# The calls for the third batch's loads moved, in pairs, between the first output stores, and ACT's token-order copies on every second quarter of an output tile

## The chip, the cores and the metric

The kernel runs on one core of a Trainium2 chip. The metric is device time in microseconds (us), lower is better; faster or slower asks for 2%. Engines: PE is TensorE (PEld its weight loads), ACT is ScalarE, DVE is VectorE, POOL is GpSimd, SP is SyncE. "ACTq" and "SPq" are the instruction queues of ACT and SP where they issue DMAs. L304 means line 304 of the kernel.

## The reference

Sliding-window attention (window 32, 8 batches, 8 heads, 576 tokens, head size 64), then two matrix products with a leaky ReLU between:

```python
scores = scale * np.matmul(q, k.transpose(0, 1, 3, 2))      # (8, 8, 576, 576)
scores = np.where(np.abs(pos[:, None] - pos[None, :]) <= 32, scores, -1e9)
attn = softmax(scores)                                      # cut: written out in the reference
x = np.matmul(attn, v).transpose(0, 2, 1, 3).reshape(4608, 512)
h = x @ w_in                                                # (4608, 2048)
out = np.maximum(0.01 * h, h) @ w_out                       # (4608, 512) float32
```

## The kernel before

Attention goes in 64 steps (8 batches x 2 halves of the tokens x 4 pairs of heads), and the two products go on beside it: a hidden group of 16 tiles (`h_tile`, 288 tokens) and output tiles (`o_tile`, 128 tokens) follow each other on TensorE, and a plan says before which hidden tile or quarter of an output tile the next attention step is put. So TensorE is fed all the time, as long as no attention step has to wait.

Parts that matter, with cuts marked by `# ...`. The loads, one buffer for each pair of heads:

```python
    def load_qk(b, p, behind=None):
        for into, src, name in ((qf, q, "qf"), (kf, k, "kf")):
            t = fload.tile([96, 2, RUN * D], FP32, name=f"{name}{p}")
            # ...
            nc.sync.dma_start(out=t, in_=src[b, p:H:NPAIR].rearrange("a (p c) d -> p a (c d)", c=RUN))
            into[b, p] = t
    # load_v(b, p): two DMAs of 144 KB, likewise on nc.sync, into vf{p}
```

The token-order copies. From batch 5 on (`BY_DMA = 5`) a DMA transposes q and k, and ACT puts the result into token order; DVE then places the keys (`place_keys`, L226):

```python
                tok = tp.rearrange("p c i -> p i c")
                if which == "q":
                    nc.scalar.activation(out=qT[b][:, p].rearrange("p (i c) -> p i c", c=RUN), in_=tok, func=AF.Copy)   # L208
                else:
                    kT = kt.tile([128, S], BF16, name="kT")
                    # ...
                    nc.scalar.activation(out=kT_v, in_=tok, func=AF.Copy)                                               # L214
                    unplaced.append((b, p, kT))
```

An attention step. `score` for step i+2: PE writes `ps` (one PSUM buffer), ACT takes the exponential `e` (L247), POOL masks it. `join(i+1)` is two small DVE instructions (L262, L264). `weighted(i)`: PE sums into `s` (L273) and multiplies into `x` (L285), DVE takes the reciprocal `r` (L291) and multiplies into `xT` (L293), which the hidden group reads:

```python
        if JOINED - 1 <= i < NC - 1:
            join(i + 1)
        place_keys()
        # ... transposes for the next batch
            score(i + 2)
        weighted(i)
        place_keys()
```

An output tile, with a hook before each quarter; ACT copies the result out of PSUM and issues the store itself:

```python
            # ... o: a PSUM tile; lo, hi: its columns, all 512 but in the last tile
            for f in range(FFC):
                if hook and lo == 0 and f % 4 == 0:
                    hook()
                nc.tensor.matmul(o[:, lo:hi], gT[:, f, ds(128 * j % RING, 128)], w_out_bf[:, f, lo:hi], ...)
            o_sb = outp.tile([128, DMODEL], FP32, name="o_sb")
            nc.scalar.activation(out=o_sb[:, lo:hi], in_=o[:, lo:hi], func=AF.Copy)      # L326
            nc.scalar.dma_start(out=out[ts(j, 128), lo:hi], in_=o_sb[:, lo:hi])          # L327
```

The plan's loop, where the change is:

```python
    for p in range(NPAIR):
        load_qk(2, p)                    # ahead of the first output tile
    # ...
    cast_v(1, 0)
    load_v(2, 0)

    def spend(us):
        nonlocal clock
        while due and due[0] <= clock:
            due.pop(0)
            i = state["done"]
            if i < 11:
                cast_v(1, i - 7)
                load_v(2, i - 7)
            step()

        b, p = state["tp"] // 8, state["tp"] % 8 // 2
        if kind == "o" and b >= BY_DMA and (b, p, "k") in qkT and state["done"] > 8 * b - 12 + p + 2:
            step_transposes(state["tp"] + 1)      # one token-order copy
            place_keys()
        clock += us
```

The framework that the kernel is written in gives DMAs issued from SP and ACT eight completion semaphores in rotation. A DMA therefore carries a wait until the eighth DMA before it has landed, counted over both engines, in the order in which the framework's scheduler expects them to issue. That is read from the built program's waits, and it concerns the program, not the chip. Below, q0, k0, v0 and so on are the third batch's loads of head pair 0 (a v load is two DMAs), and "batch 5" counts from 0.

The softmax here doesn't subtract the row's maximum and nothing guards it: scores larger than these inputs give would overflow.

Of the kernel before, what the change touches and what calls it, by code (L numbers as in the profile page):

```python
# [16 lines left out]
def kernel(  # L17
# [20 lines left out]
    NPAIR = H // 2  # L38
# [25 lines left out]
# [5 lines that stand above are left out]
            if behind is not None:  # L69
                nc.sync.dma_start(out=t[0:1, 0, 0:1], in_=behind.bitcast(FP32))  # L70
                behind = None
            nc.sync.dma_start(  # L72
                out=t, in_=src[b, p:H:NPAIR].rearrange("a (p c) d -> p a (c d)", c=RUN),
            )
            into[b, p] = t

    def load_v(b, p, behind=None):

        t = fload.tile([128, NB, D], FP32, name=f"vf{p}")
        if behind is not None:  # L80
            nc.sync.dma_start(out=t[0:1, 0, 0:1], in_=behind.bitcast(FP32))
        for a in range(2):
            nc.sync.dma_start(  # L83
                out=t[64 * a:64 * a + 64],
                in_=v[b, NPAIR * a + p].rearrange("(c p) d -> p c d", p=64),
            )
        vf[b, p] = t
# [78 lines left out]
    def cast_qk(b, p, q_eng=None):  # L166
        for eng, src, dst in ((q_eng or nc.gpsimd, qf, qb), (nc.gpsimd, kf, kb)):
            eng.tensor_copy(  # L168
                out=dst[:, p], in_=src[b, p].rearrange("p a (c d) -> p c a d", d=D),
            )  # L170

    def cast_v(b, p, on_act=False):
        for a in range(2):
            r = slice(64 * a, 64 * a + 64)
            if on_act:
                nc.scalar.activation(out=vbd[b % 2][r, p, :, r], in_=vf[b, p][r], func=AF.Copy)
            else:
                nc.gpsimd.tensor_copy(out=vbd[b % 2][r, p, :, r], in_=vf[b, p][r])  # L178


    BY_DMA = 5
    qkT = {}

    def transpose_dma(b, p):
        for which, src in (("q", qb), ("k", kb)):
            t = tdma.tile([128, RUN, 96], BF16, name=f"{which}T{p}")
            nc.sync.dma_start_transpose(out=t, in_=src[:, p].rearrange("p c a d -> p (c a d)"))
            qkT[b, p, which] = t
# [31 lines left out]
    def place_keys():  # L220

        while unplaced:
            b, p, kT = unplaced.pop(0)
            for a in range(2):
                r = slice(64 * a, 64 * a + 64)
                nc.vector.tensor_copy(  # L226
                    out=kbd[b % 2][r, p, :, r],
                    in_=kT[r].rearrange("p (n j) -> p n j", j=64),
                )
# [3 lines left out]
    def where(i):  # L233
        return i // 8, (i // 4) % 2, i % 4

    def score(i):
        b, hf, p = where(i)
        ps = scps.tile([128, 1024], FP32, name="ps")
        c0 = 512 - HALF
        for blk, q0, n in WIN[hf]:  # L240
            nc.tensor.matmul(  # L241
                ps[:, c0:c0 + n], kbd[b % 2][:, p, blk],
                qT[b][:, p, q0:q0 + n], start=True, stop=True,
            )
            c0 += n
        e = attn.tile([128, NCOL], BF16, name="e")
        nc.scalar.activation(  # L247
            out=e, in_=ps[:, 512 - HALF:512 - HALF + NCOL], func=AF.Exp, scale=scale,
        )
        pr = prob.tile([128, NCOL], BF16, name="pr")  # L250
        nc.gpsimd.tensor_mul(pr, e, mask[hf])  # L251
        probs[i] = pr, None

    def join(i):


        hf = where(i)[1]
        pr = probs[i][0]
        both = prob.tile([128, HALF], BF16, name="both")
        o0 = ODD[hf]  # L260
        o1 = o0 + NCOL - HALF
        nc.vector.tensor_add(both[:, o0:o1], pr[:, o0:o1], pr[:, HALF:NCOL])  # L262
        rest = slice(0, o0) if o0 else slice(o1, HALF)
        nc.vector.tensor_copy(out=both[:, rest], in_=pr[:, rest])  # L264
        probs[i] = pr, both

    def weighted(i):
        b, hf, p = where(i)
        pr, both = probs.pop(i)
        x = xps.tile([128, HALF], FP32, name="x")  # L270
        s = xps.tile([128, HALF], FP32, name="s")
        if both is not None:
            nc.tensor.matmul(s, ones_bd, both, start=True, stop=True)  # L273
        else:
            nc.tensor.matmul(
                s, ones_bd, pr[:, 0:HALF], start=True, stop=False, skip_group_check=True,
            )
            nc.tensor.matmul(
                s[:, ODD[hf]:ODD[hf] + NCOL - HALF], ones_bd, pr[:, HALF:NCOL],
                start=False, stop=True, skip_group_check=True,  # L280
            )
        c0 = 0
        for n_, (blk, q0, n) in enumerate(WIN[hf]):
            a = q0 - HALF * hf
            nc.tensor.matmul(  # L285
                x[:, a:a + n], vbd[b % 2][:, p, blk, :], pr[:, c0:c0 + n],
                start=(n_ == 0), stop=(n_ == len(WIN[hf]) - 1), skip_group_check=True,
            )
            c0 += n
        r = attn.tile([128, HALF], FP32, name="r")  # L290
        nc.vector.reciprocal(r, s)  # L291
        t0 = (b * S + hf * HALF) % RING
        nc.vector.tensor_mul(xT[:, p, t0:t0 + HALF], x, r)  # L293
# [45 lines left out]
    state = {"tp": 8, "done": 0}  # L339
# [12 lines left out]
    def step_transposes(upto):  # L352
        while state["tp"] < min(upto, 8 * B):
            b = state["tp"] // 8
            if b not in t_parts:
                t_parts[b] = transposes(b)
            next(t_parts[b])
            state["tp"] += 1

    def step():  # L360


        i = state["done"]
        b, r = i // 8, i % 8
# [3 lines that stand above are left out]
        if b > 0:  # L368
            upto = 8 * (b + 1) + (PLAN[b > 1][0][r] if b + 1 < BY_DMA else 0)
            step_transposes(max(upto - 1, 8 * (b + 1)))  # L370
        if i < 7:
            score(i + 1)
        elif 8 <= i < NC - 2:
            nb, _, np_ = where(i + 2)
            if nb >= BY_DMA:
                step_transposes(8 * nb + 2 * np_ + 2)
# [4 lines that stand above are left out]
        if b > 0:  # L381
            step_transposes(upto)
        if 0 < b < B - 1:
            for p in PLAN[b > 1][1][r] if b + 1 < BY_DMA else ():
                cast_qk(b + 1, p)
                if b + 2 < B:
                    load_qk(b + 2, p)

            n, p = (b + 1, 3) if r == 0 else (b + 2, r - 4)
            if p in range(4 if r == 0 else 3) and BY_DMA <= n < B:  # L390
                step_transposes(8 * (n - 1) + 2 * p + 2)
                place_keys()
                cast_qk(n, p)
                transpose_dma(n, p)
                if n + 1 < B:
                    load_qk(n + 1, p)
            for p in PLAN[b > 1][2][r]:
                cast_v(b + 1, p)
                if b + 2 < B:
                    load_v(b + 2, p)  # L400
        state["done"] += 1
# [70 lines left out]
    for f in range(FFC):  # L472
        h_tile(1, f)
        if f % 4 == 3:
            p = f // 4
# [7 lines left out]
            score(8)  # L483
    state["tp"] = 16
    score(9)
    for p in range(NPAIR):
        load_qk(2, p)



# [18 lines left out]
        due.append(prev + (at[i // 4] - LEAD + (1.2 if i < 12 else 0) - prev) * (i % 4 + 1) / 4)  # L509
    clock = 0.0  # L510
    cast_v(1, 0)
    load_v(2, 0)

    def spend(us):
        nonlocal clock
        while due and due[0] <= clock:
            due.pop(0)
            i = state["done"]
            if i < 11:
                cast_v(1, i - 7)  # L520
                load_v(2, i - 7)
            step()

        b, p = state["tp"] // 8, state["tp"] % 8 // 2
        if kind == "o" and b >= BY_DMA and (b, p, "k") in qkT and state["done"] > 8 * b - 12 + p + 2:
            step_transposes(state["tp"] + 1)
            place_keys()
        clock += us

    for us, kind, g, f in plan:  # L530
        if kind == "h":
            spend(us)
            h_tile(g, f)
        elif f == 0:
            o_tile(g, lambda: spend(O_US))
# [28 lines left out]
```

## Time and profile before

| | before |
|---|---|
| time, median of 3 runs | 336.55 us (336.29 to 337.34) |
| span of the profiled run | 336.1 us (it took 337.79 us, mean granted clock 0.990) |
| PE busy | 314.5 us (94%) |
| DVE, ACT, POOL busy | 228.3, 213.9, 180.5 us |
| PE idle between 40 and 315 us | 5.5 us in three gaps |

No engine but PE is near its limit as an average, and yet PE's few gaps are made by others. The way to read this profile is to find the gaps of PE and ask at each which instruction it waited for, and what that one stood behind. The prediction below shows those lines and how they are read.

### The profile page before, as it was taken

The page shows a single profiled execution, that of the slowest core. Times are in us where ns is not written, and L with a number is a line of the kernel's source. Part 1 is how long each engine was busy: PE and PEld are TensorE (multiplying, and loading weights), DVE is VectorE, ACT ScalarE, POOL GpSimd, SP SyncE. Part 2 cuts the span into 40 slices and gives each one's busy share as a digit, 9 for nine tenths or more (in the row PEclk, how much of TensorE's full clock was granted, in tenths as well). Part 3 has the DMA queues.
Part 4 walks back from the last instruction along what each step waited for, and adds up shares of the span by engine and source line. Part 5 has one row for each costly group of instructions (what it writes and reads, how often), then busy time and mean ns, then how long its engine had stood idle before and what let it go on. Part 6 is the DMA issues. An engine that isn't in the chain of part 4 may idle for free.

```text
span 336.1 us, 6770 instructions
## 1 busy us (share of the span) xinstructions
PE 314.5 (94%) x2581; PEld 210.8 (63%) x2581; DVE 228.3 (68%) x310; ACT 213.9 (64%) x432; POOL 180.5 (54%) x213
## 2 busy tenths in 40 slices
PE   2588999699999999999999799999999999999996
PEld 1346775376675767667675475748585666666653
DVE  5489654598777978888676867777786767666200
ACT  5775792266674756667489587878787555555441
POOL 6797767549764646659541666529741454221000
PEclk9999999799999999999999899999999999999999
DMA  8999978997695433568993289914840101010102
GB/s 187 219 196 225 269 179 187 258 196 200 186 191 169 124 71 115 150 196 154 221 184 103 82 158 226 211 50 113 145 117 34 62 2 62 2 63 3 62 2 93
DMA packets 75445, 45.93 MB, mean 137 GB/s; under 512 B 54292, under 2 KB 70932, under 8 KB 75412
## 3 DMA queue, kind: packets, MB, share of 16 engines
q1 hardware_dynamic: 65796, 31.86, 46.3%
q10 hardware_dynamic: 5328, 9.44, 8.1%
q0 software_dynamic: 4288, 4.20, 7.6%
q8 instruction: 20, 0.33, 0.4%
q14 instruction: 13, 0.11, 0.1%
HBM read 36.70 MB, written 9.44 MB: 137 GB/s over the span
## 4 chain that ended last, share of the span: by engine, by line
PE 74%; DMA 9%; DVE 5%; ACT 4%; SPq 3%; POOL 2%; issue 2%; ACTq 0%; DVEq 0%
PE mm L304 33%; PE mm L321 29%; DMA kf<-in_k_dram 9%; PE x L285 4%; PE ps L241 4%; DVE r L291 3%; PE tp L200 2%; ACT kT L214 2%; PE s L273 2%; SPq L72 2%; ACT qT L208 1%; SPq L83 1%; DVE kbd L226 1%; POOL vbd L481 1%; POOL pr L251 1%
## 5 line engine op out<-in xcount | busy, mean ns | idle before, releaser
L291 DVE RECIPROCAL r<-s 128x288 f32<-128x288 f32 x64 | 125.2, 1956 | 46.9 <-PE s L273 37.8
L251 POOL TENSOR_TENSOR pr<-e,mask 128x544 bf16<-128x544 bf16 x64 | 77.8, 1215 | 112.2 <-ACT e L247 79.5
L304 PE MATMUL mm<-xT,w_in_bf 128*128 128x288 bf16 x1024 | 135.1, 288 | 0.0
L321 PE MATMUL mm<-w_out_bf,gT 128*128 128x512 bf16 (+2 forms) x592 | 131.3, 376 | 0.0
L308 ACT ACTIVATE gT<-mm 128x288 bf16<-128x288 f32 x256 | 101.0, 415 | 23.5 <-PE mm L304 11.3
L304 PEld LDWEIGHTS <-w_in_bf 128*128 128x128 bf16 x1024 | 98.9, 98 | 25.2 <-issue 0.4
L321 PEld LDWEIGHTS <-gT 128*128 128x128 bf16 x592 | 56.6, 98 | 60.4 <-issue 1.0
L326 ACT ACTIVATE o_sb<-mm 128x512 f32<-128x512 f32 (+2 forms) x37 | 21.6, 585 | 63.9 <-PE mm L321 63.9
L247 ACT ACTIVATE e<-ps 128x544 bf16<-128x544 f32 x64 | 40.0, 624 | 25.2 <-PE ps L241 8.1
L226 DVE COPY kbd<-kT 64x576 bf16<-64x576 bf16 x64 | 28.5, 445 | 24.4 <-ACT kT L214 23.8
L178 POOL CAST vbd<-vf 64x576 bf16<-64x576 f32 x58 | 38.7, 668 | 1.9
L293 DVE TENSOR_TENSOR xT<-x,r 128x288 bf16<-128x288 f32 x64 | 29.3, 458 | 6.7
L168 POOL CAST kb<-kf 96x768 bf16<-96x768 f32 x32 | 27.8, 867 | 9.0 <-DMA kf<-in_k_dram 9.0
L241 PE MATMUL ps<-qT,kbd 128*128 128x128 bf16 (+2 forms) x320 | 27.0, 218 | 3.4 <-ACT e L247 3.4
L241 PEld LDWEIGHTS <-kbd 128*128 128x128 bf16 x320 | 21.0, 101 | 12.0 <-issue 4.5
L285 PE MATMUL x<-pr,vbd 128*128 128x128 bf16 (+2 forms) x320 | 26.4, 215 | 1.1 <-DVE xT L293 1.0
L262 DVE TENSOR_TENSOR both<-pr 128x256 bf16<-128x256 bf16 x52 | 24.4, 469 | 3.4 <-POOL pr L251 1.9
L285 PEld LDWEIGHTS <-vbd 128*128 128x128 bf16 x320 | 21.2, 100 | 6.5 <-DVE xT L293 2.8
L264 DVE COPY both<-pr 128x32 bf16<-128x32 bf16 x52 | 22.3, 428 | 0.0
L168 POOL CAST qb<-qf 96x768 bf16<-96x768 f32 x24 | 19.8, 823 | 0.0
L200 PE MATMUL tp<-ident,qb 96*128 96x96 bf16 x120 | 9.4, 220 | 8.5 <-DVE qb L168 8.5
L273 PE MATMUL s<-both,ones_bd 128*128 128x288 bf16 x52 | 14.9, 286 | 1.5 <-DVE r L291 1.5
(39 smaller groups left out, 137.9 us busy)
## 6 DMA issues: line engine op xcount, KB each, us to landing
qf<-in_q_dram SPq DMA_DIRECT2D x32, 288.0 KB, 4.2
kf<-in_k_dram SPq DMA_DIRECT2D x32, 288.0 KB, 4.4
vf<-in_v_dram SPq DMA_DIRECT2D x64, 144.0 KB, 4.5
out_dram<-o_sb ACTq DMA_DIRECT2D x35, 256.0 KB, 2.3
w_in_bf<-in_moe_w_in_dram POOLq DMA_DIRECT2D x8, 256.0 KB, 6.6
w_out_bf<-in_moe_w_out_dram POOLq DMA_DIRECT2D x4, 512.0 KB, 12.0
qT<-qb SPq DMA_TRANSPOSE x12, 3.8
kT<-kb SPq DMA_TRANSPOSE x12, 3.8
```

The costliest lines, as they stand in the source:

```text
L168: eng.tensor_copy(out=dst[:, p], in_=src[b, p].rearrange("p a (c d) -> p c a d", d=D),)
L178: nc.gpsimd.tensor_copy(out=vbd[b % 2][r, p, :, r], in_=vf[b, p][r])
L226: nc.vector.tensor_copy(out=kbd[b % 2][r, p, :, r], in_=kT[r].rearrange("p (n j) -> p n j", j=64),)
L241: nc.tensor.matmul(ps[:, c0:c0 + n], kbd[b % 2][:, p, blk], qT[b][:, p, q0:q0 + n], start=True, stop=True,)
L247: nc.scalar.activation(out=e, in_=ps[:, 512 - HALF:512 - HALF + NCOL], func=AF.Exp, scale=scale,)
L251: nc.gpsimd.tensor_mul(pr, e, mask[hf])
L285: nc.tensor.matmul(x[:, a:a + n], vbd[b % 2][:, p, blk, :], pr[:, c0:c0 + n], start=(n_ == 0), stop=(n_ == len(WIN[hf]) - 1), skip_group_c ...
L291: nc.vector.reciprocal(r, s)
L293: nc.vector.tensor_mul(xT[:, p, t0:t0 + HALF], x, r)
L304: nc.tensor.matmul(h[:, 0:HALF], w_in_bf[:, c, ts(f, 128)], xT[:, c, ds(t0, HALF)], start=(c == 0), stop=(c == DMC - 1),)
L308: nc.scalar.activation(out=gT[:, f, ds(t0, HALF)], in_=h[:, 0:HALF], func=AF.Prelu, alpha=0.01,)
L321: nc.tensor.matmul(o[:, lo:hi], gT[:, f, ds(128 * j % RING, 128)], w_out_bf[:, f, lo:hi], start=(f == 0), stop=(f == FFC - 1),)
```

## The change

The intent: the third batch's q and k loads, eight DMAs in one burst just ahead of the first output stores, are to be issued a pair at a time between these stores; and ACT's token-order copies, so far one before every quarter of an output tile, come before every second one, so that ACT's other work fits in between. No instruction is added or taken away.

```diff
--- before.py
+++ after.py
@@ -483,8 +483,6 @@
             score(8)
     state["tp"] = 16
     score(9)
-    for p in range(NPAIR):
-        load_qk(2, p)
 
 
 
@@ -509,20 +507,25 @@
         due.append(prev + (at[i // 4] - LEAD + (1.2 if i < 12 else 0) - prev) * (i % 4 + 1) / 4)
     clock = 0.0
     cast_v(1, 0)
-    load_v(2, 0)
+    turn = 0
 
     def spend(us):
-        nonlocal clock
+        nonlocal clock, turn
         while due and due[0] <= clock:
             due.pop(0)
             i = state["done"]
             if i < 11:
                 cast_v(1, i - 7)
-                load_v(2, i - 7)
+
+            if i < 12:
+                load_qk(2, i - 8)
             step()
+            if 10 <= i < 14:
+                load_v(2, i - 10)
 
         b, p = state["tp"] // 8, state["tp"] % 8 // 2
-        if kind == "o" and b >= BY_DMA and (b, p, "k") in qkT and state["done"] > 8 * b - 12 + p + 2:
+        turn += 1
+        if kind == "o" and turn % 2 and b >= BY_DMA and (b, p, "k") in qkT and state["done"] > 8 * b - 12 + p + 2:
             step_transposes(state["tp"] + 1)
             place_keys()
         clock += us
```

## The prediction

> **What bounds the kernel now.** I read the busy rows of the page first, then the windows, then the timeline at each place where TensorE stands still. PE is 314.5 us busy in a span of 336.1, so only its idle time and its slow time can be won. The sliced rows say where they are (busy tenths of 8.4 us slices; PEclk is the granted clock in tenths):
>
> ```profile
> PE   2588999699999999999999799999999999999996
> ...
> PEclk9999999799999999999999899999999999999999
> ```
>
> Three dips: the start (before 40 us), slices 7 and 22, and the last slice. The change touches neither the start nor the end. The windows (us, then busy us with counts of PE, PEld, DVE, ACT, POOL, then PEclk, DMA share, GB/s) size the two in the middle, and a third, small one:
>
> ```profile
> 58.00:60.00 2.00, 1.82 (x10) 0.71 (x8) 1.90 (x2) 0.00 (x0) 1.72 (x3) 1.00 1.08 240
> 60.00:62.00 2.00, 0.00 (x0) 0.00 (x0) 0.41 (x1) 0.17 (x1) 0.00 (x0) 1.00 1.07 286
> 62.00:64.00 2.00, 1.49 (x16) 1.01 (x16) 0.83 (x1) 1.08 (x2) 1.40 (x2) 0.94 1.09 319
> 64.00:66.00 2.00, 2.00 (x6) 0.71 (x5) 1.59 (x2) 0.60 (x1) 1.86 (x3) 0.50 1.25 198
> ...
> 186.00:188.00 2.00, 0.96 (x8) 0.45 (x7) 1.96 (x5) 1.27 (x3) 0.67 (x1) 1.00 0.35 131
> 188.00:190.00 2.00, 0.77 (x8) 0.45 (x8) 1.90 (x3) 0.62 (x1) 1.63 (x2) 1.00 0.35 131
> 190.00:192.00 2.00, 2.00 (x11) 1.26 (x9) 2.00 (x3) 0.78 (x2) 2.00 (x4) 0.51 0.03 8
> ...
> 224.00:226.00 2.00, 1.75 (x12) 0.77 (x10) 1.90 (x2) 0.69 (x2) 1.21 (x1) 1.00 0.32 117
> ```
>
> Each large gap is paid twice: PE idles, and then runs some 3.4 us at half clock. **Gap A** (60 us): 2.69 us idle, and 8 of the 128x512 matmuls take 2.92 us where 16 take 3.45 (so 8 take 1.73): 1.2 lost there and about 0.5 in the small ones around, 1.7 in all; sum 4.4 us. **Gap B** (187 us): idle 0.74 + 1.24 + 0.28 = 2.26, and 28 matmuls of 128x288 take 5.10 us instead of 3.43, 1.67 lost; sum 3.9. **Gap C** (226 us): 0.25 + 0.28 = 0.53. Nothing else of size lies between 40 and 315 us, so 336.55 - 4.4 - 3.9 - 0.5 = 327.7 us is the floor of this change.
>
> The timeline gives A's cause (start, duration, instruction, idle before it and what ended it):
>
> ```profile
> 54.89 0.40 SPq L72 DMA_DIRECT2D kf<-in_k_dram  x1
> ...
> 61.39 0.34 ACTq L327 DMA_DIRECT2D out_dram<-o_sb  x1
> 61.83 0.62 ACT L247 ACTIVATE e<-ps 128x544 bf16<-128x544 f32 x1 [4.25 <-DMA kf<-in_k_dram]
> 62.51 0.40 PE L241 MATMUL ps<-qT,kbd 128*128 128x64 bf16 x5 [2.69 <-ACT e L247]
> ```
>
> ACT finished copying output tile 1 at 57.58 but issued its store at 61.39; the chain of work shows the kf load issued at 54.89 landing at 61.31. ACT's next exponential stood behind the store, and PE behind that. B's cause:
>
> ```profile
> 184.52 1.17 ACT L214 ACTIVATE kT<-kT 128x576 bf16<-128x576 bf16 x1
> ...
> 185.71 0.91 DVE L226 COPY kbd<-kT 64x576 bf16<-64x576 bf16 x2 [1.23 <-ACT kT L214]
> ...
> 186.94 1.95 DVE L291 RECIPROCAL r<-s 128x288 f32<-128x288 f32 x1
> ...
> 188.94 0.28 PE L273 MATMUL s<-both,ones_bd 128*128 128x288 bf16 x1 [1.24 <-DVE r L291]
> ```
>
> The eight token-order copies of batch 5 come on every quarter of output tiles 15 and 16. The last kT copy ends at 185.69; DVE takes its key copies in order ahead of the reciprocal, whose sums had been ready since 182.88.
>
> **What the Trainium skill says.** "TensorE: Matmul & The Clock Gate", Part 1: an idle window halves the clock, some 3.4 us of activity restores it. The trace agrees on the half (0.50, 0.51) and the length, but shows it after gaps of only 2.7 and 2.3 us. The same page (architectural detail, on queue depths) has ScalarE and VectorE as strict FIFO: both gaps show it, the exponential behind a store, the reciprocal behind a key copy. "ScalarE: Activation LUTs", on what ACT_TABLE_LOAD costs, gives 186 ns + 0.833 ns per element, 666 ns for 576: the copies from PSUM take 0.65 to 0.67, but the strided ones from SBUF take 1.18 here, so I use 1.18 (1.08 from start to start). "DMA: Bandwidth & Descriptors", on issuing engines not being separate queues: loads from SP and stores from ACT share 16 engines. The DMA share stays near or above 1 from 54 to 72 us.
>
> **The change, part by part.** No instruction is added or removed; only orders change.
>
> *Copies.* A quarter tile is 4 x 0.216 = 0.86 us of PE; with a step of attention a tile takes about 4.3. Up to the exponential after tile 16, ACT now has 8 copies x 1.08 + one exponential 0.6 + two output copies with their stores 2 x 1.05 = 11.3 us of work, in the 7.5 us from 174.84 to 182.35; from 174.84 this ends at 186.2, and that exponential did start at 186.63. With every second quarter the odd turns fall on the first and third quarter of each tile (16 turns per hidden group keep the parity): two copies a tile. Then it is 4 x 1.08 + 0.6 + 2.1 = 7.0 us in 7.5, and ACT waits for PE. DVE's key copy is then done before 183.3, the reciprocal runs 183.3 to 185.3 and the multiply behind it ends at 185.8, some 1.5 us before the next hidden group needs it at about 187.3. I followed the plan through all tiles: batches 5, 6 and 7 take tiles 15-18, 19-22 and 23-26; no copy is forced by a score, and no transpose waits for a tile not yet read. Over three tiles ACT has 9.8 us of work in 11.7. Gaps B and C go: 3.9 + 0.5 = **4.4 us**.
>
> *Loads.* The intent is that stores do not stand behind a burst of loads. What the store waits for is a semaphore: in the instruction list of the built kernel before, SP's and ACT's DMAs share eight completion semaphores in rotation, so each waits until the eighth before it has landed, in the order in which the scheduler expects them to issue. There the second store's eighth-before is the k load of pair 1 (issued 54.89), exactly what the trace shows. But moving a call later in the source does not hold SP back: the q and k buffers were free long ago, and a small program built apart showed SP's loads listed ahead of work emitted before them. So q0 k0 q1 k1 q2 k2 keep their places; only v0 (two DMAs) now comes before q3 k3. In the old list, q and k loads are 1.1 us apart, v loads 1.65, counted in PE work. With k2 at 30.2 on that scale this puts v0 at 31.3 and 32.95, q3 34.6, k3 35.7, the next v 36.8; the stores keep 32.2 and 36.3. The eighth before the second store is then: k3, q3, v0b, first store, v0a, k2, q2, **k1 again**. On the chip k1 has the same bytes ahead of it and should again land near 61.3. **Gap A stays: 0 us.** The later v loads are needed from 83 us on and land before.
>
> Sum: 336.55 - 4.4 = **332.1 us**, 1.3% faster.
>
> **Rivals.** (1) *Both parts work*, as the author means: 327.7. For it: the wait in A is a matter of order alone, and a k3 listed 0.7 us later than I reckon would move the second store's wait to q1, landing about 1.3 us earlier, perhaps with no throttling: about 329. Against it: nothing gates SP. (2) *The second store's wait moves the wrong way*, to q2 (if the next v load comes 0.5 us earlier than reckoned): A grows by about 1.3 us, 333.4. (3) *The copies move the stall*: two copies just before each hidden group could delay its activations. Four PSUM tiles rotate there, and ACT is at 84% over these tiles, so I expect under 0.5 us. (4) *Late v loads stall GpSimd's casts*: pairs 2 and 3 of v are now queued behind batch 3's q and k, but would land some 80 and 86 us in, before casts at 88 and later: nothing.
>
> **Range and chances.** Three quarters on 332.1 within 1 us; about 15% on A being gone or shortened (327.7 to 329.6); the rest on A longer or a copy stall. Faster by over 2% means under 329.82, which needs A's help. I choose 329.4 to 333.8.
>
> **What would show it.** Right: gap A still there at 60 to 62.5 us, with a store issued as a kf load lands and half clock after it; no PE gap at 187 and 226; PEclk 1.00 there; ACT's copies in twos with an output copy between. Wrong: PE continuous through 60 us, the second store at about 57.6. The loads' step would then be the one that failed: the semaphore order, or SP's running ahead. A new PE gap at the start of a hidden group (tiles 17, 21, 26) would refute the copies' step.

## The result

| | before | changed |
|---|---|---|
| median | 336.94 us (336.29 to 338.48, 4 runs) | 332.50 us (332.14 to 333.43, 4 runs) |
| span of the profiled run | 336.1 us | 330.7 us |
| PE busy | 314.5 us | 312.2 us |

The ratio is 0.9866 (95% interval 0.9825 to 0.9907): 1.3% faster, which counts as the same at 2%. Ratios here and below are the mean time of one kernel's fast runs over the mean of the other's in the same rounds, so they are not quite the ratio of the medians.

The profile after, first the two sliced rows of the page:

```profile
PE   2588999799999999999999999999999999999996
...
PEclk9999999899999999999999999999999999999999
```

The dip in slice 22 (counted from 0, at 187 us) is gone, the one in slice 7 (at 60 us) is still there. The windows of the changed kernel at the same places (us, then busy us with counts of PE, PEld, DVE, ACT, POOL, then PEclk, DMA share, GB/s):

```profile
60.00:62.00 2.00, 0.30 (x2) 0.02 (x1) 0.78 (x2) 0.30 (x1) 0.33 (x1) 1.00 1.22 199
62.00:64.00 2.00, 1.62 (x14) 1.11 (x14) 0.95 (x1) 0.95 (x2) 1.53 (x2) 0.73 1.09 276
64.00:66.00 2.00, 2.00 (x6) 0.73 (x5) 1.46 (x2) 0.60 (x1) 1.86 (x3) 0.50 1.09 273
...
186.00:188.00 2.00, 2.00 (x24) 1.58 (x22) 1.68 (x6) 1.32 (x3) 0.00 (x0) 1.00 0.02 8
188.00:190.00 2.00, 2.00 (x19) 1.61 (x17) 1.90 (x3) 1.85 (x6) 1.76 (x2) 1.00 0.35 126
...
224.00:226.00 2.00, 2.00 (x25) 1.70 (x23) 2.00 (x4) 1.67 (x5) 1.96 (x3) 1.00 0.11 21
```

PE is busy throughout at 186 to 190 us (gap B) and 224 to 226 us (gap C), and at full clock. At 60 us (gap A) it still stands, and half clock follows. The timeline of the changed kernel at gap A:

```profile
53.83 0.40 SPq L72 DMA_DIRECT2D kf<-in_k_dram  x1
...
55.62 2.72 SPq L83 DMA_DIRECT2D vf<-in_v_dram  x2
...
57.70 0.40 PE L241 MATMUL ps<-qT,kbd 128*128 128x96 bf16 x5 [0.53 <-ACT e L247]
...
58.93 0.32 SPq L72 DMA_DIRECT2D qf<-in_q_dram  x1
60.04 0.32 SPq L72 DMA_DIRECT2D kf<-in_k_dram  x1
61.26 0.34 ACTq L327 DMA_DIRECT2D out_dram<-o_sb  x1
61.70 0.62 ACT L247 ACTIVATE e<-ps 128x544 bf16<-128x544 f32 x1 [3.56 <-DMA kf<-in_k_dram]
62.38 0.40 PE L241 MATMUL ps<-qT,kbd 128*128 128x64 bf16 x5 [2.08 <-ACT e L247]
```

It is the same picture as before: output tile 1 was copied at 58.14, its store was issued at 61.26, and what ended the wait was the landing of the k load issued at 53.83 (at 61.2). The second output store stands behind the k load of pair 1, as in the kernel before. The 0.53 us at 57.70 belong to it too: the first store was issued at 56.55, after a wait for a v load, with an exponential behind it. In all PE stands idle for 2.66 us between 40 and 75 us, against 2.69 in the kernel before. All that the moved lines did is visible in SP's queue: the two v loads now come ahead of the q and k loads of pair 3. The loads of pairs 0 to 2 were issued back to back as before. And gap B, in the same view:

```profile
181.06 1.16 ACT L214 ACTIVATE kT<-kT 128x576 bf16<-128x576 bf16 x1
...
182.28 0.90 DVE L226 COPY kbd<-kT 64x576 bf16<-64x576 bf16 x2
...
183.48 0.62 ACT L247 ACTIVATE e<-ps 128x544 bf16<-128x544 f32 x1 [0.47 <-ACT o_sb L326]
183.50 1.95 DVE L291 RECIPROCAL r<-s 128x288 f32<-128x288 f32 x1
...
185.56 0.46 DVE L293 TENSOR_TENSOR xT<-x,r 128x288 bf16<-128x288 f32 x1
...
186.87 3.59 PE L304 MATMUL mm<-xT,w_in_bf 128*128 128x288 bf16 x28
```

The key copies on DVE end at 183.18, the reciprocal follows after a short join at 183.50 instead of 186.94, and the multiply is done at 186.02, 0.85 us before the hidden group starts. 28 matmuls of the hidden group now take 3.59 us; in the kernel before the same line shows 5.26 us, at half clock.

### The profile page after: what moved, and what is told of

Read it like the earlier page. It is cut to its first block, busy times and chain, and to the rows that moved or that the text cites. A ratio compares the mean times of both kernels' runs of the same rounds, so it can differ in the third digit from the quotient of the medians.

```text
span 330.7 us, 6770 instructions
## 1 busy us (share of the span) xinstructions
PE 312.2 (94%) x2581; PEld 209.8 (63%) x2581; DVE 230.5 (70%) x310; ACT 213.9 (65%) x432; POOL 180.2 (54%) x213
## 4 chain that ended last, share of the span: by engine, by line
PE 81%; DMA 9%; POOL 2%; DVE 2%; SPq 2%; ACT 1%; issue 1%; ACTq 0%; DVEq 0%; POOLq 0%
PE mm L321 35%; PE mm L304 34%; DMA kf<-in_k_dram 9%; PE x L285 4%; PE ps L241 4%; PE tp L200 2%; PE s L273 2%; DVE r L291 2%; SPq L72 1%; SPq L83 1%; POOL vbd L481 1%; POOL pr L251 1%; POOL kb L168 0%; DVE xT L293 0%; PE mm L334 0%
## 5 line engine op out<-in xcount | busy, mean ns | idle before, releaser
L304 PE MATMUL mm<-xT,w_in_bf 128*128 128x288 bf16 x1024 | 133.4, 286 | 0.0
L262 DVE TENSOR_TENSOR both<-pr 128x256 bf16<-128x256 bf16 x52 | 25.2, 485 | 3.7 <-POOL pr L251 2.4
L264 DVE COPY both<-pr 128x32 bf16<-128x32 bf16 x52 | 23.8, 458 | 0.0
```

The source lines that it names most:

```text
L304: nc.tensor.matmul(h[:, 0:HALF], w_in_bf[:, c, ts(f, 128)], xT[:, c, ds(t0, HALF)], start=(c == 0), stop=(c == DMC - 1),)
```

## The experiments

Eight kernels, each an edit of the kernel before or of the changed one. Runs 1 to 4 were made on one chip with a common set of runs before (median 336.47 us); runs 5 to 7 share nearly the same set (336.38); run 8 came in later rounds, in which the kernel before took 338.06 us. All edits keep the result correct.

**1. Copies alone.** The kernel before, with the second part of the change only.

```diff
+        turn += 1
-        if kind == "o" and b >= BY_DMA and ...
+        if kind == "o" and turn % 2 and b >= BY_DMA and ...
```

> Only the copies' part of the change (every second quarter tile), the loads as before. My theory: the copies are worth all of the gain, about 4.4 us (gap B 3.9 with its half-clock time, gap C 0.5), so the same time as the changed kernel, about 332.3 us, 1.3% under before; TensorE without idle time at 186-190 and 225-226 us, but still idle some 2.7 us at 60 us. Rival: the two parts need each other or share the gain, then this run keeps 2 us or more of it back (334 us or more).

Measured: 332.60 us median (331.35 to 335.01, 6 runs), ratio 0.9893 (0.9853 to 0.9933), 3.6 us by that ratio. Between 40 and 325 us, PE's idle time with a named releaser is a single line:

```profile
62.87 0.61 PE L241 MATMUL ps<-qT,kbd 128*128 128x64 bf16 x5 [2.60 <-ACT e L247]
```

Gaps B and C are gone, A is there. Its median is within 0.1 us of the changed kernel's, though that was timed with other rounds. The copies account for the gain.

**2. Loads alone.** The changed kernel, with the copies on every quarter again.

```diff
-        if kind == "o" and turn % 2 and b >= BY_DMA and ...
+        if kind == "o" and b >= BY_DMA and ...
```

> Only the loads' part of the change, copies on every quarter as before. My theory: worth nothing, since SP issues the q and k loads of pairs 0 to 2 as early as before and the second output store still waits for the k load of pair 1: within 0.4 us of before, TensorE still idle 2 to 2.7 us at 60 us. Rival: the loads' part brings 1 us or more by itself (335.5 us or less).

Measured: 336.70 us (336.27 to 337.53, 6 runs), ratio 1.001 (0.9981 to 1.0038). The loads' part brings nothing. The main idle lines of PE in its profile:

```profile
61.22 0.40 PE L241 MATMUL ps<-qT,kbd 128*128 128x64 bf16 x5 [0.54 <-ACT e L247]
...
68.46 0.28 PE L273 MATMUL s<-both,ones_bd 128*128 128x288 bf16 x1 [0.77 <-DVE r L291]
69.03 0.41 PE L285 MATMUL x<-pr,vbd 128*128 128x64 bf16 x5 [0.28 <-DVE xT L293]
186.06 0.40 PE L241 MATMUL ps<-qT,kbd 128*128 128x64 bf16 x5 [0.73 <-ACT e L247]
187.70 0.28 PE L273 MATMUL s<-both,ones_bd 128*128 128x288 bf16 x1 [1.24 <-DVE r L291]
188.26 0.41 PE L285 MATMUL x<-pr,vbd 128*128 128x64 bf16 x5 [0.28 <-DVE xT L293]
```

Gap B is that of the kernel before, to 0.01 us. At gap A the line expected to show 2 to 2.7 us shows 0.54: the k load of pair 1 had landed early, at 60.1. But the idle time has only moved. With the 1.05 us at 68 us, where DVE now holds PE, and smaller pieces at 48.58, 55.25 and 64.47 us, PE stands idle for 2.66 us between 40 and 75 us, as in the changed kernel, against 2.69 before. So one line does not size a gap; its neighbourhood has to be summed. The sum and the six timed runs both say that the loads' part is worth nothing.

**3. The v load first.** The changed kernel, with `load_v(2, 0)` ahead of the q and k loads. It has to wait for a cast on POOL, so SP really does hold the loads behind it.

```diff
     cast_v(1, 0)
+    load_v(2, 0)
     turn = 0
-            if 10 <= i < 14:
+            if 11 <= i < 14:
                 load_v(2, i - 10)
```

> The changed kernel with one move: the first v load of the third batch is issued ahead of its q and k loads again (as in the kernel before). It has to wait for a cast on GpSimd, so it holds the loads behind it on SP, and in the built program the second output store then shares its semaphore with a v load of batch 2 that landed by about 56 us. Same bytes. My theory (the store waits for a semaphore, nothing else): the second store issues when its tile is copied, about 57.6 us; the idle time at 60 us and the half clock after it go, 4.4 us under the changed kernel: about 328.1 us. Rival (a full DMA ring or busy engines hold the store up, whatever its semaphore): store and gap stay at 61 us, 332.5 us.

Measured: 328.92 us (328.08 to 329.63, 6 runs), ratio 0.9778 (0.9748 to 0.9807), so 2.2% under before; the verdict is "unclear" because the interval's upper end lies above 0.98. The timeline and the windows:

```profile
56.13 0.58 SPq L72 DMA_DIRECT2D qf<-in_q_dram  x1
...
57.59 0.34 ACTq L327 DMA_DIRECT2D out_dram<-o_sb  x1
58.13 0.62 ACT L247 ACTIVATE e<-ps 128x544 bf16<-128x544 f32 x1 [0.57 <-POOL vbd L178]
...
60.00:62.00 2.00, 1.85 (x19) 1.09 (x17) 1.90 (x3) 0.62 (x1) 1.86 (x4) 1.00 1.06 321
...
64.00:66.00 2.00, 2.00 (x11) 0.94 (x10) 1.90 (x3) 0.00 (x0) 1.22 (x1) 1.00 1.11 254
```

The first q load is issued at 56.13 instead of 52.17, the second store at 57.59, and gap A is gone. (The expectation's "batch 2" is the second batch.) From 40 to 325 us only 0.36 us of idle time with a named releaser are left. Against the copies alone of the same rounds (means 328.99 and 332.80) it is worth 3.8 us; 4.4 were expected.

**4. The first four stores from SP.** The changed kernel; ACT no longer waits for a DMA, and each store holds back the loads behind it in SP's queue.

```diff
-            nc.scalar.dma_start(out=out[ts(j, 128), lo:hi], in_=o_sb[:, lo:hi])
+            (nc.sync if j < 4 else nc.scalar).dma_start(out=out[ts(j, 128), lo:hi], in_=o_sb[:, lo:hi])
```

> The changed kernel with the stores of output tiles 0 to 3 issued from SP instead of ACT, so that ACT can't stand behind them and the loads behind each store are really held back in between. My theory: gap at 60 us and half clock gone, about 328 us, as with the v load first. Rival (the loads now come late for the casts of the third batch, or o_sb buffers free late): 1 to 3 us given back between 65 and 95 us, 329 to 331 us.

Measured: 328.86 us (328.00 to 329.59, 6 runs), ratio 0.9773 (0.9744 to 0.9802), again "unclear". In SP's queue only pair 0's loads now come before the second store (57.78 us); those of pair 1 follow it, from 58.23. This is what the change's first part was meant to do, and it has the same effect as run 3. Nothing was given back between 65 and 95 us that the time would show. Runs 3 and 4 are the best versions found; their medians lie some 3.6 us under the changed kernel's, which was timed in other rounds.

**5. Filling the gaps.** The kernel before, with matmuls that nobody reads in place of the idle time. They shorten no wait, they only keep PE busy.

```diff
+            if i in (10, 36):
+                keep_busy(10 if i == 10 else 8)
             step()
```

> The kernel before, with matmuls whose result nobody reads put where TensorE stands idle: 10 (2.2 us) ahead of the step at gap A, 8 (1.7 us) ahead of the step at gap B. They shorten no wait; they only keep TensorE busy. My prediction reckoned that each gap is followed by a half clock that costs 1.7 us: then this gains 3.3 us, 333.2. Rival, from the clocks listed beside the runs of before (1.0, 0.995 and 0.99 all occur): the half clock comes only in some runs and costs about 1.1 us on average, so about 335.4 us, with the runs closer together and clocks at 1.0.

Measured: 335.51 us (335.09 to 335.64, 6 runs), ratio 0.9969 (0.9939 to 1.0), about 1.0 us. The six runs lie within 0.6 us, those of before within 3.1. The windows behind both gaps:

```profile
64.00:66.00 2.00, 1.85 (x17) 1.04 (x16) 1.68 (x2) 0.60 (x1) 1.86 (x3) 1.00 1.32 160
...
190.00:192.00 2.00, 2.00 (x19) 1.60 (x17) 2.00 (x2) 1.64 (x4) 1.94 (x4) 1.00 0.14 29
```

In this profile the clock stays at 1.00 (one of the six timed runs lists a mean of 0.995). The half clock is real, but the prediction charged it to every run at both gaps, 3.3 us in all, and on average it costs less. The fillers took somewhat more than the idle time that they replaced: 3.9 us of them and 2.2 us of idle time left between 40 and 230 us, against 5.5 us of idle time before. So an estimate of the cost is the 1.0 us gained, and up to 0.6 us more. The mean clocks listed for the twelve runs of before in these rounds fall short of 1 by 0.0036 on average, which over 335 us is 1.2 us (also an estimate). And the times of these runs go with their clocks: six with a mean clock of 0.999 or more took 335.75 us on average, six with 0.990 to 0.995 took 336.99.

**6. Keys behind the reciprocal.** The kernel before, with ACT's queue untouched; from batch 5 on DVE's key copies come after the step's reciprocal and multiply.

```diff
             join(i + 1)
-        place_keys()
+        if b < 4:
+            place_keys()
...
             step_transposes(state["tp"] + 1)
-            place_keys()
```

> The kernel before, copies on every quarter, but from batch 5 on VectorE's key copies are put behind the reciprocal and the multiply of the step instead of ahead of them. ACT's queue is unchanged. My theory (two things hold TensorE at gap B: 0.74 us the exponential late on ACT, 1.5 us the reciprocal behind the key copies on VectorE): only some 0.74 us idle left at 186-190 us and none at 226; 2 to 3 us under before, about 334. Rival (ACT's backlog alone sets the gap): no change, within 0.5 us of before.

Measured: 333.55 us (332.89 to 334.69, 6 runs), ratio 0.9917 (0.9886 to 0.9948), 2.8 us. The timeline at gap B:

```profile
182.39 1.96 DVE L291 RECIPROCAL r<-s 128x288 f32<-128x288 f32 x1 [1.18 <-PE s L273]
...
184.83 2.78 DVE L226 COPY kbd<-kT 64x576 bf16<-64x576 bf16 x6
186.10 0.62 ACT L247 ACTIVATE e<-ps 128x544 bf16<-128x544 f32 x1 [0.47 <-PE mm L321]
186.78 0.40 PE L241 MATMUL ps<-qT,kbd 128*128 128x64 bf16 x5 [0.73 <-ACT e L247]
```

The reciprocal starts as soon as its sums are there, and of gap B only the 0.73 us of the late exponential remain, as expected. At gap C 0.28 us were left where none was expected. So gap B had two causes from one backlog: 0.74 us directly on ACT, 1.5 us on DVE, whose queue had been given ACT's late output ahead of urgent work.

**7. Even quarters.** The changed kernel, with the copies on the second and fourth quarter of each tile.

```diff
-        if kind == "o" and turn % 2 and b >= BY_DMA and ...
+        if kind == "o" and turn % 2 == 0 and b >= BY_DMA and ...
```

> The changed kernel with the copies on the second and fourth quarter of each tile instead of the first and third: same number per tile, but the last one is queued 0.9 us closer to the hidden group that follows. My theory (the rate of two per tile is what matters, with about 1.5 us to spare): same as the changed kernel, 332.6 within 0.6 us. Rival (position matters: the copy just ahead of a hidden group delays its activations or the multiply): 1 us or more slower, TensorE idle at the start of the hidden groups near 187, 206 and 226 us.

Measured: 331.87 us (331.13 to 333.01, 6 runs), ratio 0.9868 (0.9837 to 0.9898), the same as the changed kernel's 0.9866. PE has no gap at the start of a hidden group. The rate of two copies to a tile is what counts; their place in it does not show.

**8. Turning the rotation.** Run 3 let the loads start later, so it also lightened the traffic at 57 us. This run leaves the loads of pairs 0 to 2 alone and only shifts which DMA is the eighth before the second store, from the k load of pair 1 to that of pair 2.

```diff
                 load_qk(2, i - 8)
+            if i == 10:
+                for n in range(4):
+                    t = const.tile([1, 1], FP32, name=f"tiny{n}")
+                    nc.sync.dma_start(out=t, in_=q[0, 0, 0:1, n:n + 1])
```

> The changed kernel with four loads of 4 bytes each on SP, right behind the k load of pair 2. They move no data worth the name and nobody reads them; they only turn the rotation of the eight semaphores, so that in the built program the second output store waits for the k load of pair 2 instead of pair 1. In the run with the v load first the traffic at 57 us was lighter too; here it is the same as in the changed kernel. My theory (the semaphore alone decides): the second store issues as that load lands, two loads or about 2.7 us later, near 64 us; TensorE idle 4.5 us or more at A; about 335.3 us. Rival (busy DMA engines or a full ring hold the store): unchanged, store near 61.3 us, 332.5 us.

Measured: 333.96 us (332.13 to 335.18, 6 runs) where before took 338.06: ratio 0.988 (0.9836 to 0.9925), 0.0014 above the changed kernel's, some 0.5 us, well inside the intervals. The time tells nothing apart. The chain of work does (start, duration, what):

```profile
55.46 7.08 DMA kf<-in_k_dram
...
62.62 0.34 ACTq L327
```

The store was released as the k load of pair 2, issued at 55.46, landed at 62.55. The k load of pair 1, issued at 54.48, had landed 6.1 us later, at 60.6: the store stayed where it was for two more microseconds with that one done. Which landing the store waits for thus follows the rotation. The size missed. The rotation gave the first v load a new partner too, k1, and the small loads ahead of it had waits of their own, so that it was issued at 60.63 instead of 55.62; the k load of pair 2 then landed 7.1 us after its issue, against 9.4 in the changed kernel. PE's idle time ahead of the step's scores grew from 2.08 to 3.05 us, and all of it between 40 and 75 us from 2.66 to 4.74, but this profile shows no half clock behind it.

## Why the prediction was right

- **The sum.** Predicted 332.1 us, inside 329.4 to 333.8, same; measured 332.5 and a ratio of 0.9866, same. It was reached by the steps given, with one term of the wrong size, and that it came within 0.4 us is in part luck (see the half clock).
- **Copies: right, to a few tenths on the timeline.** ACT was reckoned to wait for PE there, and it did: the output copy, at 182.42, ended a wait for PE, and the exponential followed at 183.48. The reciprocal was put at 183.3 to 185.3 and ran 183.50 to 185.45; the end of the multiply was put at 185.8 and came at 186.02. The slack ahead of the hidden group was put at 1.5 us and was 0.85, since the group itself started earlier (186.87 for 187.3). Run 6 confirms both causes of gap B apart, run 1 that this part carries the whole gain.
- **Loads: right.** The order of the DMAs in the changed program is the one worked out in advance, down to v0, the first store, v0, q3, k3 and the second store (the built program lists it so), and the second store waited for k1 again. Run 2 measured the part by itself as nothing. Runs 3 and 8 show that the store's release follows the semaphore: give it another partner and it issues when that one has landed.
- **Half clock: the mis-sized term.** "Each large gap is paid twice" was read from a single profile, and from one of the longer executions: it took 337.79 us at a mean clock of 0.990, as low as any listed, while the sum starts from the median of 336.55. The prediction counted 1.67 us of half clock in what the copies win and 3.3 at both gaps; run 5 and the listed clocks put both together at some 1.0 to 1.6 us on average (estimates), because it does not come in every run. The two measurements of the copies, 3.6 us (run 1) and 4.5 us (changed kernel, 0.9866 of 337.17), lie on either side of the predicted 4.4. The idle time of gaps B and C alone is 2.8 us; how much of the rest is half clock is not resolved by intervals of that width. Nor is it resolved why run 3 won 3.8 us over run 1 and not 4.4: in the profiles it has 2.3 us less idle time, and the mean clocks listed for the two (0.999 and 0.997) leave some 0.6 us for the half clock (an estimate), less than was measured.
- **Rivals.** "Both parts work" would have needed the loads to be held back; runs 3 and 4 do hold them, and land at 328.9 where 327.7 was named as the floor. The rival that copies would stall hidden groups fell with run 7. Late v loads cost nothing seen: in the changed kernel POOL waited once for a v load, 0.2 us. The wait moving to a later load did not happen by itself; run 8 forced it to k2, one load past the q2 named, and its cost stayed too small for the intervals.
- **Open.** The idle time between 40 and 75 us is 2.66 to 2.69 us in four profiles (before, changed, runs 1 and 2) but 3.40 and 3.10 in runs 6 and 7. Why, and why it comes in one piece or in several, no run here tells. Nor is it shown why the half clock follows a gap of 2.1 us in one run and not one of 3.05 in another.

## What to carry to other kernels

Moving a DMA's call later in the source delays nothing if nothing in its queue makes it wait: give it something to wait for (a buffer, a cast, or a store ahead of it in the same queue), and read from the built program which earlier DMA each store's semaphore belongs to. A compute engine that issues stores puts its next computation behind whatever those stores wait for; move such stores to a queue that has nothing urgent. And when one engine hands its output to another in order, spread it at the rate at which both have room: eight copies in two tiles cost 2.3 us of idle TensorE, two to a tile cost none, though no engine's average load changed by more than two points.

## What the Trainium skill lacked or had wrong

- "TensorE: Matmul & The Clock Gate", Part 1, has the clock halved after at least one idle window of about 3.4 us. In four profiles here (before, changed, copies alone, even quarters) it went to 0.50 to 0.58 after PE had stood for only 2.1 to 2.7 us at gap A, and in two after 2.3 us in three pieces at gap B. After 0.5 and 1.2 us it did not, and in one profile not after 3.05 us either. The page calls the window free-running, which fits a half clock that comes by chance; what it lacks is that a single gap shorter than the window can be enough, and the mean cost, here some 1.0 to 1.6 us for two such gaps (an estimate from run 5 and the listed clocks).
- "DMA: Bandwidth & Descriptors", on issuing engines not being separate DMA queues, says that issuing from several engines saves only the sequencer's issue time. The page does say, in its part on the anatomy of one DMA, that the issuing sequencer takes the wait for a semaphore. It lacks what follows for a compute engine: while its DMA waits, the computation behind it waits too. In the kernel before ACT stood 3.8 us behind one store; run 4, the changed kernel with four stores moved to SP, took 328.9 us, where the copies alone took 332.6 in the same rounds.
- "SBUF — State Buffer" says that an access which crosses to a new 16-byte line pays a penalty; no page has what a strided source costs ScalarE. The same token-order copy of 128x576 elements took a median of 0.65 us out of PSUM (batches 0 to 4) and 1.18 us out of SBUF (1.15 to 1.20, batches 5 to 7). No run tells what part of it is the stride and what the memory.
